# A decode-layer backward kernel: six V slots of its own, reloaded once their V is transposed, and more side-product steps per head after head 52

## The chip, the cores and the metric

The kernel runs on one core of a Trainium2 chip. The metric is device time in microseconds (us) of that core. Each kernel was run several times; executions of one kernel mostly agree within 0.3%, and comparisons carry a 95% interval.

## The reference, cut to what matters

The reference is one transformer layer at decode (one query per sequence) with its gradients: layer norm, attention over a cache of 4096 keys, output projection, gated MLP. There are 4 x 32 = 128 heads, and each has a K and a V of 4096 x 128 in bfloat16, 1 MiB each. What counts here is the backward part of attention:

```python
q = (x @ wq).reshape(B, Sq, H, Dh).transpose(0, 2, 1, 3)
scores = einsum("bhqd,bhkd->bhqk", q, k_cache) * Dh**-0.5
p = softmax(scores); o = einsum("bhqk,bhkd->bhqd", p, v_cache)
# gradients, per head (dO is the gradient of o, c = sum(dO * o)):
#   grad_V = outer(p, dO)                                1 MiB out
#   dP = V @ dO                                          V is read a second time
#   grad_K = outer(p * (dP - c) * scale, q)              1 MiB out
# side products: gradients of wq, wo, w1, w2, w3 and x, some 15 MB out
```

So the backward part moves 1 MiB in and 2 MiB out per head, and little arithmetic goes with it.

## The kernel before

On-chip memory holds 22 slots of 128 x 4160 bfloat16, kept in a queue `free`. Every large thing takes the slot at the head of the queue and gives it back at the tail when the program order is done with it; the framework adds the waits.

```python
class Slot:
    def __init__(self, name):
        self.i = free.popleft()
        self.t = slotp.tile([P, SLOT], BF16, name=name, tag=f"slot{self.i}")
    def give(self):
        free.append(self.i)
```

In the backward loop TensorE transposes a V in four groups of eight blocks, ScalarE evicts them, and TensorE makes dP. VectorE makes the outer products; GpSimd issues the stores, SyncE the loads:

```python
def V_T(s, ps):
    VTs[s] = Slot("VT")
    VT, Vn = VTs[s].heads(), V2s[s].heads()
    for g in range(SJ // GW):                       # 4 groups
        pt = ps.tile([P, GW, P], BF16, tag="tps", name="pt_tps")
        for i in range(GW):
            nc.tensor.transpose(pt[:, i, :], Vn[:, g * GW + i, :], ident_b[:])
        nc.scalar.copy(out=VT[:, g * GW:(g + 1) * GW, :], in_=pt[:])
    V2s.pop(s).give()

def load_V2():
    s = nv["next"]
    if s < NH:
        V2s[s] = Slot("V2")
        nc.sync.dma_start(out=V2s[s].heads(), in_=cache_head(A_v_cache, s))
        nv["next"] += 1

def front(s):                                       # cut
    ...
    V_T(s, psT)
    for j in range(SJ):
        nc.tensor.matmul(dP_ps[:, j:j + 1], lhsT=VT[:, j, :], rhs=dOT_bf[:, s:s + 1], start=True, stop=True)
    VTs.pop(s).give()
    P_pairs(s + 1)                                  # a copy on GpSimd

def grad_V(s):
    gv = Slot("gv")
    outer(gv.heads(), P2s.pop(s), reps["rdo", s // REP][:, s % REP, :])     # VectorE
    nc.gpsimd.dma_start(out=rows_of(out_3[b, h]), in_=gv.heads())
    gv.give()
# grad_K(s): dSt, dS2 on VectorE, then gk in the same way to out_2

def prefetch(s):
    while nv["next"] < min(NH, s + 10) and len(free) > 8:
        load_V2()

for s in range(NH):
    prefetch(s + 1)
    if s + 1 < NH:
        if s + 1 not in V2s and s + 1 not in VTs:
            load_V2()
        front(s + 1)
        grad_V(s + 1)
    grad_K(s)
    if s < S0:                                      # S0 = 8
        step("o")                                   # rest of dO
    else:
        step("s", 1 if s < S0 + 44 else 2 + (s % 4 == 0))     # side products
step("s", 400)
```

The side products are a generator; one step is one small matmul with its eviction, and every eighth or so a store. A part of it:

```python
oflat = Slot("oflat")
for b in range(B):
    nc.gpsimd.dma_start(out=oflat.b(HD)[b:b + 1, :], in_=O_sb[b::B, :])     # four tiny transfers
for _ in range(6):
    yield
for h0 in range(0, H, 8):                           # grad of wo, uses oflat
    ...
```

## Time and profile before

| | before |
|---|---|
| time, median of the first three runs | 1743.66 us |
| profiled execution | 1740.73 us (span 1739.0) |
| bytes moved | 707.86 MB, mean 407 GB/s |
| backward loop | from about 720 us to the end |
| TensorE, VectorE, ScalarE busy | 76%, 72%, 55% |

How to read what follows. "DMA" is a row of tenths (busy share of the 16 DMA engines per slice), "GB/s" what they moved. A line of the view of stretches names a stretch in us from the start, its length, busy time of TensorE, weight loads, VectorE, ScalarE and GpSimd with counts, and at the end the granted TensorE clock, the DMA share and GB/s. A line of the view of waits reads: engine and line that waited, what it waited for, total us, how often, the longest. A line of the issues names the transfer, its queue, how many, the size, and the median us from issue to landing. The prediction below shows the views of the kernel before.

### The profile page before, as it was taken

Reading aid. Unit: us, or ns where it says so; the run is one execution under the profiler, and the core shown is the slowest. Engines: PE = TensorE matmul, PEld = TensorE weight load, DVE = VectorE, ACT = ScalarE, POOL = GpSimd, SP = SyncE. Lnnn points to the kernel's source line nnn. Section 1 sums busy time; section 2 is a strip of 40 time slices with the busy share of each in tenths; the row PEclk is TensorE's granted clock in tenths of the full one; section 3 lists DMA queues with packets and bytes.
Section 4 is the critical chain, followed back from the end, with each engine's and each line's share of the span. In section 5 each row is a group of like instructions: output and inputs, shape, how many; then the busy total and the mean of one; then the engine's idle time right before and its main releaser. Section 6 shows DMA issues by size and latency. Waiting matters only on the chain.

```text
span 1739.0 us, 44055 instructions
## 1 busy us (share of the span) xinstructions
PE 1321.9 (76%) x18996; PEld 1113.4 (64%) x18996; DVE 1250.8 (72%) x1385; ACT 955.6 (55%) x1464; POOL 508.2 (29%) x815
## 2 busy tenths in 40 slices
PE   5889888888888888888777767777577667656675
PEld 4667666676666667777667666655466455545564
DVE  5989999889998996675666576656566465656665
ACT  3455445444444444765545445576367566656675
POOL 2333333333333331231222232212223232223332
PEclk8999999999999999765655565586555655656555
DMA  9999999999999999799999999999999999999998
GB/s 398 410 419 418 419 418 419 419 413 418 419 414 399 417 406 396 312 403 421 420 420 416 419 419 413 408 423 423 413 389 396 409 401 409 403 413 403 415 407 328
DMA packets 107043, 707.86 MB, mean 407 GB/s; under 512 B 11024, under 2 KB 18840, under 8 KB 23904
## 3 DMA queue, kind: packets, MB, share of 16 engines
q1 hardware_dynamic: 66880, 422.60, 59.9%
q0 software_dynamic: 39968, 282.44, 39.3%
q8 instruction: 149, 2.44, 0.5%
q14 instruction: 46, 0.38, 0.1%
HBM read 422.58 MB, written 282.34 MB: 405 GB/s over the span
## 4 chain that ended last, share of the span: by engine, by line
DMA 37%; DVE 9%; issue 5%; PE 5%; ACT 4%; POOL 2%; DVEq 0%; POOLq 0%; ACTq 0%; SPq 0%
DMA out_dram<-gv 21%; DMA out_dram<-gk 13%; DVE gk L1091 5%; DVE gv L1091 3%; ACT VT L759 3%; PE pt_tps L758 2%; POOL P L1075 2%; DMA out_dram<-gwq 1%; DMA wo<-in_A_wo_dram 1%; DMA V<-in_A_v_cache_dram 1%; PE gps L886 0%; PE dP_ps L1085 0%; DVE PK L421 0%; PE rep_ps L1063 0%; DVE dS L1112 0%
## 5 line engine op out<-in xcount | busy, mean ns | idle before, releaser
L759 ACT COPY VT<-pt_tps 128x1024 bf16<-128x1024 bf16 x512 | 492.7, 1015 | 247.6 <-PE pt_tps L758 166.7
L758 PE MATMUL pt_tps<-ident_b,V 128*128 128x128 bf16 x4096 | 453.9, 294 | 122.2 <-ACT VT L759 119.1
L758 PEld LDWEIGHTS <-V 128*128 128x128 bf16 x4096 | 402.5, 138 | 202.1 <-issue 180.7
L1091 DVE TENSOR_TENSOR gv<-P,reps 128x4096 bf16<-128x4096 bf16 x128 | 292.9, 2289 | 198.2 <-DMA out_dram<-gv 141.0
L1091 DVE TENSOR_TENSOR gk<-dS,reps 128x4096 bf16<-128x4096 bf16 x128 | 293.4, 2292 | 145.2 <-DMA out_dram<-gv 86.7
L421 DVE TENSOR_TENSOR PK<-Kn,PK 128x4096 bf16<-128x4096 bf16 x128 | 302.9, 2366 | 35.2 <-POOL PK L417 34.8
L436 PE MATMUL M_ps<-PK,Vn 128*128 128x130 bf16 x4096 | 285.9, 222 | 42.6 <-DMA Vn<-in_A_v_cache_dram 42.5
L436 PEld LDWEIGHTS <-Vn 128*128 128x128 bf16 x4096 | 253.2, 99 | 62.6 <-DMA Vn<-in_A_v_cache_dram 55.3
L328 DVE STREAM_TRANSPOSE KT<-Kn 128x512 f32<-128x512 f32 (+1 forms) x321 | 250.9, 798 | 0.5 <-issue 0.5
L323 ACT COPY KT<-pt_tps 128x1024 bf16<-128x1024 bf16 x128 | 129.4, 1012 | 187.1 <-PE pt_tps L322 154.7
L1085 PE MATMUL dP_ps<-dOT_bf,VT 128*128 128x1 bf16 x4096 | 146.5, 166 | 107.8 <-DVE dSt L1109 55.8
L1085 PEld LDWEIGHTS <-VT 128*128 128x128 bf16 x4096 | 139.1, 104 | 121.5 <-ACT VT L759 60.7
L1116 POOL DMA_DIRECT2D out_dram<-gk x128 | 68.2, 532 | 429.2 <-DVE gk L1091 414.0
L417 POOL COPY PK<-P_all 128x64 bf16<-128x64 bf16 x128 | 32.3, 252 | 437.0 <-ACT P_all L411 411.8
L336 POOL COPY zq<-qT_bf 128x2 bf16<-128x2 bf16 x128 | 152.1, 1189 | 0.0
L1102 POOL DMA_DIRECT2D out_dram<-gv x128 | 68.5, 535 | 269.0 <-DVE dSt L1109 251.7
L1075 POOL COPY P<-P_all 128x64 bf16<-128x64 bf16 x128 | 133.8, 1046 | 0.0
L411 ACT COPY P_all<-pt_P 32x64 bf16<-32x64 bf16 x256 | 51.9, 203 | 57.5 <-PE pt_P L407 55.3
L322 PE MATMUL pt_tps<-ident_b,Kn 128*128 128x128 bf16 x1024 | 80.6, 223 | 0.7 <-DVE qrep L282 0.7
L446 PE MATMUL kP_ps<-PK,onesw 128*32 128x512 bf16 x1024 | 79.6, 388 | 0.0
L322 PEld LDWEIGHTS <-Kn 128*128 128x128 bf16 x1024 | 62.2, 100 | 26.5 <-issue 26.4
L400 ACT ACTIVATE Pn<-E,rl 128x1024 bf16<-128x1024 f32 x64 | 73.7, 1151 | 2.8 <-DVE rl L397 2.8
(227 smaller groups left out, 1299.8 us busy)
## 6 DMA issues: line engine op xcount, KB each, us to landing
Kn<-in_A_k_cache_dram SPq DMA_DIRECT2D x128, 1024.0 KB, 14.8
Vn<-in_A_v_cache_dram SPq DMA_DIRECT2D x128, 1024.0 KB, 14.9
V<-in_A_v_cache_dram SPq DMA_DIRECT2D x128, 1024.0 KB, 13.5
out_dram<-gv POOLq DMA_DIRECT2D x128, 1024.0 KB, 15.9
out_dram<-gk POOLq DMA_DIRECT2D x128, 1024.0 KB, 16.2
wq<-in_A_wq_dram SPq DMA_DIRECT2D x8, 1024.0 KB, 12.6
out_dram<-gw POOLq DMA_DIRECT2D x6, 896.0 KB, 19.3
wo<-in_A_wo_dram SPq DMA_DIRECT2D x4, 1024.0 KB, 12.0
```

The costliest lines, as they stand in the source:

```text
L322: nc.tensor.transpose(pt[:, i, :], Kn[:, c * GW + i, :], ident_b[:])
L323: nc.scalar.copy(out=KT[:, c * GW:(c + 1) * GW, :], in_=pt[:])
L328: nc.vector.transpose(out=KT[:, c * w_:(c + n) * w_], in_=Kn[:, c * w_:(c + n) * w_])
L336: nc.gpsimd.tensor_copy(out=zq[gi % 2][hl][:, 32:132:67], in_=qT_bf[:, s:s + 1].to_broadcast([P, 2]))
L421: nc.vector.tensor_tensor(out=PK[:, :, 0:Dh].rearrange("p j (r t) -> p j r t", t=2), in0=Ks[s].heads().rearrange("p j (r t) -> p j r t", t=2),
L436: nc.tensor.matmul(hold["M"][:], lhsT=Vn[:, j, :], rhs=PK[:, j, :], start=(j == 0), stop=(j == SJ - 1))
L446: nc.tensor.matmul(hold["kP"][32 * q:32 * (q + 1), :, :], lhsT=ones_window(w), rhs=PK[:, j0:j0 + 4, 0:Dh], start=(w == 0 and c == 0), stop ...
L758: nc.tensor.transpose(pt[:, i, :], Vn[:, g * GW + i, :], ident_b[:])
L759: nc.scalar.copy(out=VT[:, g * GW:(g + 1) * GW, :], in_=pt[:])
L1075: nc.gpsimd.tensor_copy(out=P2s[s][:], in_=P_all[:, s, :, None].to_broadcast([P, SJ, 2]))
L1085: nc.tensor.matmul(dP_ps[:, j:j + 1], lhsT=VT[:, j, :], rhs=dOT_bf[:, s:s + 1], start=True, stop=True)
L1091: nc.vector.tensor_tensor(out=dst.rearrange("p j (r t) -> p j r t", t=2), in0=col2[:, :, None, :].to_broadcast([P, SJ, Dh // 2, 2]), in1=r ...
```

## The change

The intent: a V should be loaded as soon as an earlier V has been transposed, not when some output store has left a slot. So six slots become a ring for V alone, and all others rotate among outputs. The step rate of the side products rises from 2.25 to 2.75 per head after head 52, so that they end earlier.

```diff
     class Slot:
-        def __init__(self, name):
-            self.i = free.popleft()
+        def __init__(self, name, src=free):
+            self.i = src.popleft()
             self.t = slotp.tile([P, SLOT], BF16, name=name, tag=f"slot{self.i}")
@@ V_T
-        V2s.pop(s).give()
+        sl = V2s.pop(s)
+        (vring if len(V2s) + len(vring) < NV2 else free).append(sl.i)
@@
+    NV2 = 6
+    vring = deque()
     nv = {"next": 0}
     def load_V2():
         s = nv["next"]
         if s < NH:
-            V2s[s] = Slot("V2")
+            V2s[s] = Slot("V2", vring if vring else free)
@@
-        def prefetch(s):
-            while nv["next"] < min(NH, s + 10) and len(free) > 8:
+        def prefetch():
+            while nv["next"] < NH and vring:
                 load_V2()
@@
-            prefetch(s + 1)
+            prefetch()
@@
-                step("s", 1 if s < S0 + 44 else 2 + (s % 4 == 0))
+                step("s", 1 if s < S0 + 44 else 2 + (s % 4 < 3))
```

## The prediction

> **What bounds the kernel now.** I read the page first. Its second part shows DMA at nine tenths in nearly every slice while no compute engine is near full, so the 16 DMA engines are the bound; the interest is in the row below, what they moved. The total is 707.86 MB, and the change moves the same bytes. The slices are 43.5 us each; the backward loop over heads starts in the 17th (about 720 us).
>
> ```profile
> DMA  9999999999999999799999999999999999999998
> GB/s 398 410 419 418 419 418 419 419 413 418 419 414 399 417 406 396 312 403 421 420 420 416 419 419 413 408 423 423 413 389 396 409 401 409 403 413 403 415 407 328
> ```
>
> The first row cannot rank the slices; the second can: about 420 GB/s when the queues are full, 389 to 409 in most slices from the 30th on, 328 in the last. So the engines count as busy while some of them have nothing to take. I then cut the backward part into stages (view of chosen stretches; last three columns are granted clock, DMA share, GB/s):
>
> ```profile
> 720.00:760.00 40.00, 31.91 (x507) 28.86 (x506) 30.57 (x25) 29.36 (x32) 14.51 (x19) 0.63 0.91 362
> 760.00:1240.00 480.00, 356.44 (x4487) 323.80 (x4484) 296.09 (x246) 270.33 (x297) 123.70 (x185) 0.59 1.01 419
> 1240.00:1660.00 420.00, 282.70 (x3384) 225.19 (x3383) 256.73 (x216) 254.46 (x319) 123.10 (x170) 0.57 1.00 404
> 1660.00:1740.00 80.00, 53.55 (x666) 44.07 (x663) 47.63 (x40) 49.97 (x61) 21.71 (x31) 0.56 0.89 359
> ```
>
> The stage of 480 us is at the DMA limit already. The other three are below it, and what can be won lies there. Why they are below is in the waits of the load queue (whole run), where line 768 is the second load of V:
>
> ```profile
> SPq L768 <- DMA out_dram<-gk: 510.3, 49, 38.7
> SPq L768 <- DMA out_dram<-gw: 116.3, 5, 24.6
> SPq L768 <- DMA out_dram<-gv: 115.4, 14, 23.0
> SPq L768 <- DMA out_dram<-gwq: 67.6, 3, 24.6
> SPq L768 <- PE pt_tps L758: 20.5, 19, 6.0
> ```
>
> A V load waits some 810 us in all for an output store to leave the slot it is given, and only 20.5 us for the transposes of an earlier V. The longest wait, 38.7 us, is at the start: between 720 and 740 us the DMA view has no read at all and moves 6.67 MB. The compute side waits for the same stores (view of waits, whole run):
>
> ```profile
> DVE gv L1091 <- DMA out_dram<-gv: 141.0, 35, 7.7
> DVE gk L1091 <- DMA out_dram<-gk: 52.0, 26, 2.4
> ACT VT L759 <- DMA out_dram<-gk: 42.6, 10, 12.6
> ACT gw L880 <- DMA out_dram<-gk: 26.1, 5, 10.2
> ```
>
> The VectorE waits cost nothing while other stores are still being moved. The ScalarE ones can: when ScalarE stands 12.6 us for a VT slot, nothing is produced behind it. In the timeline this one ends at 1398.9 us; the next stores are issued only from 1405 us, and the DMA strip of 1400 to 1420 us falls to 371 GB/s.
>
> **What the Trainium skill says.** "DMA: Bandwidth & Descriptors", section on the anatomy of one DMA (SWDGE path): DMA engines do not wait on semaphores; any wait happens on the issuing sequencer before dispatch. The trace agrees: the waits above stand on the queue of SyncE, and a V load that waits holds up those behind it. Same page, "Issuing engines are not separate DMA queues": loads from SyncE and stores from GpSimd share the 16 engines and interleave. It agrees: between 1120 and 1240 us the two together make 423 GB/s, where loads alone made 418 to 419 in the forward part: no second path. Same page, "Specifications": a fabric ceiling of 435 GB/s and an HBM limit per core of about 358. The trace stays below the first and contradicts the second (407 GB/s mean), so 420 is near the most there is. "Perfetto Trace Analysis", "Optimization Strategy": repeated bubbles on the engine that should be full can mean too few buffers. Here they do: 22 slots are shared.
>
> **The change part by part.** No instruction and no byte is added or removed; the forward part and the first eight V loads stay the same. So everything before about 725 us is unchanged.
>
> 1. *The V ring.* I followed the slot lists of both programs in program order. Before, the rule "more than 8 free" keeps nine slots in rotation, and from head 8 on over half of the V loads (66 of 115) get a slot whose last user was an output store; in heads 0 to 7 the rule lets only one V be loaded (the ninth), with four more just before head 8. After, every load from the ninth on takes the slot of a V that has been transposed, five to six heads ahead. The 810 us of waits of the load queue should nearly go. By themselves they are not time: they count where the engines starved.
> 2. *The output slots.* Before, an allocation of gv or gk that has to wait for a store has some 3.5 to 4 younger stores behind it. After, the slots outside the ring all rotate, and that number is about 2 in heads 0 to 7 (worse than 2.7), 3.7 in heads 8 to 15 (equal), 5 in 16 to 35, and 6 to 9 afterwards. So when a wait ends, 6 to 9 MB are still on the way (14 to 21 us at 421 GB/s) where it was 4 MB (10 us). That covers a stop like the 6 us between wait and next store above.
> 3. *Side products.* The step rate goes from 2.25 to 2.75 per head from head 52. The last gwo takes its slot at head 109 instead of 121, so the last heads have only their own work. Per head the rate adds half a step, about 0.3 us of ScalarE (590 ns per gwo eviction). ScalarE per head: 4 x 1.015 us for VT, 0.3 for reps, 2.75 x 0.55 for steps = 5.9 us. VectorE: 2 x 2.29 + 0.245 + 0.226 = 5.05 us. DMA: 3 x 1.0486 MB at 421 GB/s = 7.5 us. There is room, so this part is not a cost.
>
> Sum, by stage. The DMA time lost is stretch x (1 - rate / full rate):
> - 720 to 760: 40 x (1 - 362/421) = 5.6 us lost. The ninth load waits until the third V is transposed, some 8 to 10 us in, and output slots are tight. I take 3 us back.
> - 760 to 1240: at 419, nothing (the best part of it made 423; deeper queues might give 1 to 3 us).
> - 1240 to 1660: 420 x (1 - 404/419) = 15 us lost. Some stays: the stretch 1260 to 1280 has 1923 packets under 2 KB, and loads of weights still wait in the same queue. I take 11 to 12 us back.
> - 1660 to the end of the stores (1732): 28.7 MB in 72 us, 68 us at 421. In this tail each head took about 6.4 us with the gwo steps, against 2.1 MB / 421 = 5 us of stores. Without steps I expect about 5.3 us (the rate of the first heads: 7 gk in 40 us is 5.7 with other side work), and a backlog of 8 stores hides the rest. I take 4 us back.
> Together 18 to 19 us, plus about 2 for the deeper queue in the middle: 1743.7 - 21 = 1722 us.
>
> **Rivals.**
> A. *Full saturation.* From 720 us to the end 414 MB are moved (406 GB/s x 1020 us). At 422 to 425 throughout, they take 974 to 981 us; against 1012 used, that is 31 to 38 us less: 1706 to 1713. For it: 423 over 120 us, and the last stores alone run at about 430 (5.26 MB in the 12.3 us after 1720). Against: the early heads and the small packets.
> B. *Output slots become the bound early.* With six slots tied to V, eight held by the M sums and three by wo, four are left for VT, gv and gk in heads 0 to 7, and seven until head 13 or so. A gk waits for the gv of one head before. With a store of L us from issue to landing, and one gv and one gk (4.6 us) per step, a head takes about (L + 4.6) / 2: 7.5 us needs L = 10.4. Stores took 5.6 us there without reads and 15 to 18 with full queues. If the ring's reads stretch L to 14, a head takes 9.3 us, 1.8 us too much over some 8 heads: 15 us lost, and the time would be about 1737. Against it: if the engines starve, L shrinks, so it corrects itself.
> C. *The reads were hidden anyway.* The engines are full through most of it, and if the bubbles after 1240 us come from side products taking slots rather than from V, only start and tail are won: 7 us, 1737.
> D. *Compute takes over.* TensorE runs at a granted clock of 0.5 to 0.6 and takes turns with ScalarE on the transposes. At 6.4 us per head in the tail and half a step more, about 6.9, it stays under 7.5. I hold this unlikely.
>
> **Range and chances.** Main line 1722; A pulls to 1708, B and C to 1737. I take 1709 to 1736. Faster by over 2% needs less than about 1709, 35 us won, hardly without A in full: 0.08. Slower by over 2% has no mechanism of that size: 0.01. Within: 0.91.
>
> **What would show it.** Right: the load queue's waits for out_dram fall from about 810 to under 100 us and turn to TensorE's transposes; reads appear before 735 us; the stretch that was 404 is at 415 or more; the last 70 us before the end keep above 415; stores take longer from issue to landing (20 us or more instead of 16). Wrong: the stretch after 1240 stays near 404 (C); the first 60 us of the loop fall under 380 with VectorE waiting for gv (B); the DMA share falls under 0.95 in the middle (D).

## The result and the profile after

The changed kernel took 1736.69 us (median of 4 runs, 1734.48 to 1739.39), the kernel before 1743.98 us (median of 4, 1742.89 to 1746.05). The ratio is 0.9958, 95% interval 0.994 to 0.9975. The gain is real and small, about 7 us where 21 were predicted. In two more rounds of runs, both on one chip (e0 and e16 below), the same kernel came to 0.9983 (0.9964 to 1.0003) and 0.9972 (0.9953 to 0.999). So it is worth 3 to 7 us, and 1736.69 lies just above the stated range.

The profiled execution of the changed kernel took 1739.39 us, the slowest of its four, and that of before 1740.73, faster than its timed ones. The two traces therefore differ by less than the kernels do; I use them for where time moved. First the page's rows of the changed kernel:

```profile
DMA  9999999999999999899999999999999999999997
GB/s 397 410 418 418 419 418 419 419 412 418 418 415 397 418 407 396 321 388 416 414 413 415 417 412 416 422 423 423 419 412 418 414 414 414 373 400 408 410 419 315
```

The slices of 389 to 409 that began with the 30th are gone up to the 34th, as meant: from the 19th to the 34th slice the rate is 412 to 423. After that come one hole (373, the 35th), three slices of 400 to 410, and a last slice of 315. By stage, in the same stretches as in the prediction:

```profile
720.00:760.00 40.00, 29.62 (x379) 26.48 (x378) 26.72 (x22) 26.76 (x29) 13.75 (x17) 0.54 0.96 384
760.00:1240.00 480.00, 364.24 (x4620) 328.56 (x4620) 312.67 (x266) 274.95 (x304) 127.58 (x194) 0.59 1.01 415
1240.00:1660.00 420.00, 298.01 (x3573) 235.68 (x3572) 248.87 (x204) 273.85 (x347) 110.28 (x167) 0.58 1.00 408
1660.00:1740.00 80.00, 33.07 (x471) 30.25 (x468) 44.51 (x36) 28.18 (x30) 16.76 (x28) 0.57 0.85 350
```

The start gained (362 to 384), the middle lost (419 to 415), the stage after 1240 us gained a third of what was expected (404 to 408), and the last one moved less (359 to 350). Then the load queue, whole run (cut to these lines; waits of the forward part and of the program's end are left out):

```profile
SPq L773 <- PE pt_tps L758: 835.1, 116, 19.8
SPq L925 <- DMA out_dram<-gv: 23.0, 2, 15.3
SPq L502 <- DMA out_dram<-gk: 16.1, 1, 16.1
SPq L925 <- DMA out_dram<-gk: 13.9, 1, 13.9
```

Line 773 is the V load (768 before). It waits for TensorE's transposes and for no store; the three waits for stores are those of weight loads. So the mechanism works as told. The stores have a deeper backlog; the time from issue to landing in the kernel before and in the changed one:

```profile
out_dram<-gv POOLq DMA_DIRECT2D x128, 1024.0 KB, 15.9
out_dram<-gk POOLq DMA_DIRECT2D x128, 1024.0 KB, 16.2
```

```profile
out_dram<-gv POOLq DMA_DIRECT2D x128, 1024.0 KB, 24.5
out_dram<-gk POOLq DMA_DIRECT2D x128, 1024.0 KB, 24.0
```

Some 8 us longer: more stores are on the way. Counted in the trace from issues and landings, 7.4 of GpSimd's transfers are under way on average from 1340 to 1490 us, where it was 4.4. And GpSimd, which issues them, now waits for earlier stores to land (view of waits of GpSimd; the largest such wait before was 5.2 us in total):

```profile
POOL out_dram L1107 <- DMA out_dram<-gv: 53.2, 21, 4.7
POOL out_dram L1121 <- DMA out_dram<-gk: 49.3, 20, 4.1
POOL out_dram L1121 <- DMA out_dram<-gv: 26.8, 9, 4.7
POOL out_dram L1107 <- DMA out_dram<-gk: 13.1, 6, 4.1
```

The program's waits tell why: its transfers take eight semaphores in turn, so each of GpSimd's transfers waits for the eighth one back. In both traces the stores' semaphores (99 to 106) come round in order, and never more than eight of GpSimd's transfers are under way.

Last the end of both traces, the DMA strip of 1720 to 1740 us (half a microsecond per digit), before and after:

```profile
DMA  9998989999999999999899999411000000000000
```

```profile
DMA  9999899797664533323111000000000000000000
```

Before, all engines stop together. After, they fall out one by one over some 6 us. The trace has sixteen landings for each transfer, one per DMA engine, without the engine's number. Those of the last store:

| last store lands (us) | first engine | mean of 16 | last engine |
|---|---|---|---|
| before | 1732.8 | 1733.4 | 1735.1 |
| changed | 1723.4 | 1727.5 | 1733.7 |

The mean engine is done 5.9 us earlier, the last one 1.4 us. The experiments below turn on this.

A second thing is in the trace's packet records. A packet of 8192 bytes mostly takes 309 ns (16 engines at that pace make 424 GB/s). From 1340 to 1500 us the mean load packet took 350.7 ns before and 314.9 after (my reading: the loads no longer start into empty queues). But the mean store packet went from 312.4 to 320.0 ns, and of all stores from 720 us on, 743 packets (329 before) took over 550 ns, with a median of 606. Summed over the loop and divided by 16 engines, what packets of 8192 bytes took above 309 ns is, in us:

| | loads | stores | together |
|---|---|---|---|
| before | 17.2 | 12.8 | 30.0 |
| changed | 5.2 | 22.8 | 28.0 |

The loads gave back 12 us, and the stores took 10 of them.

### The profile page after: what moved, and what is told of

Same layout as the page of the kernel before. It is cut to its first block, busy times and chain, and to the rows that moved or that the text cites. A ratio compares the mean times of both kernels' runs of the same rounds, so it can differ in the third digit from the quotient of the medians.

```text
span 1737.6 us, 43932 instructions
## 1 busy us (share of the span) xinstructions
PE 1324.3 (76%) x18996; PEld 1114.6 (64%) x18996; DVE 1252.8 (72%) x1385; ACT 955.0 (55%) x1464; POOL 493.6 (28%) x815
## 4 chain that ended last, share of the span: by engine, by line
DMA 43%; DVE 5%; ACT 4%; PE 3%; issue 2%; POOL 1%; POOLq 0%; DVEq 0%; ACTq 0%
DMA out_dram<-gk 20%; DMA out_dram<-gv 18%; ACT VT L759 3%; DMA V<-in_A_v_cache_dram 3%; DVE gk L1096 2%; DVE gv L1096 2%; PE pt_tps L758 2%; DMA out_dram<-gw 2%; DMA oflat<-O_sb 1%; PE gps L891 1%; POOL P L1080 0%; PE dP_ps L1090 0%; ACT reps L1071 0%; PE rep_ps L1068 0%; ACT gwo L885 0%
## 5 line engine op out<-in xcount | busy, mean ns | idle before, releaser
L1090 PE MATMUL dP_ps<-dOT_bf,VT 128*128 128x1 bf16 x4096 | 152.1, 166 | 73.4 <-ACT VT L759 63.5
L1080 POOL COPY P<-P_all 128x64 bf16<-128x64 bf16 x128 | 119.2, 932 | 0.0
## 6 DMA issues: line engine op xcount, KB each, us to landing
out_dram<-gv POOLq DMA_DIRECT2D x128, 1024.0 KB, 24.5
```

The costliest lines, as they stand in the source:

```text
L1080: nc.gpsimd.tensor_copy(out=P2s[s][:], in_=P_all[:, s, :, None].to_broadcast([P, SJ, 2]))
```

## The experiments

My theory after the result had two parts: compute and issue stalls that are left in the changed kernel (a hole at 1500 us), and a limit of the engines with deep store queues. The rivals were that the gain came from the tail alone, or that the depth itself does harm. Each row below has 5 or 6 timed runs, but for e14 (4) and e12 (2); "before" is the kernel before on the same chip.

| run | edit | median us | before | ratio (95%) |
|---|---|---|---|---|
| e1_ring_only | ring, old step rate | 1735.91 | 1743.23 | 0.9960 (0.9945 to 0.9974) |
| e2_side_only | old rule, new step rate | 1743.17 | 1743.23 | 0.9994 (0.998 to 1.0008) |
| e3_oflat16 | oflat used 16 steps later | 1739.56 | 1743.23 | 0.9975 (0.9963 to 0.9988) |
| e4_thin_compute | changed, a quarter of the transposes | 1729.40 | 1743.23 | 0.9923 (0.9909 to 0.9938) |
| e0_after_again | changed kernel | 1741.33 | 1743.52 | 0.9983 (0.9964 to 1.0003) |
| e5_park4 | 11 output slots for 15 | 1738.79 | 1743.52 | 0.9970 (0.9958 to 0.9982) |
| e6_threes | V loads by threes | 1738.02 | 1743.52 | 0.9971 (0.9958 to 0.9984) |
| e7_ring3 | ring of 3 | 1745.26 | 1743.52 | 1.0003 (0.999 to 1.0016) |
| e8_oflat_sp | e3, tiny loads from SyncE | 1735.42 | 1744.63 | 0.9949 (0.9936 to 0.9962) |
| e10_thin_before | before, a quarter of the transposes | 1731.93 | 1744.63 | 0.9931 (0.9916 to 0.9945) |
| e12_quarter_V | e4, a quarter of each V loaded | 1511.44 | 1744.63 | 0.8664 (0.8648 to 0.8681) |
| e13_ring_late | e8, ring from head 52 on | 1737.62 | 1743.86 | 0.9963 (0.9951 to 0.9976) |
| e14_thin_ring_late | e13, a quarter of the transposes | 1728.93 | 1743.86 | 0.9912 (0.9897 to 0.9927) |
| e16_after_third | changed kernel | 1737.31 | 1742.85 | 0.9972 (0.9953 to 0.999) |
| e17_oflat_sp_again | e8 | 1736.27 | 1742.85 | 0.9961 (0.9945 to 0.9977) |
| e15_shallow_end | e8, 6 output slots from head 108 | 1738.13 | 1742.85 | 0.9968 (0.9955 to 0.9981) |

**e1_ring_only and e2_side_only** do one part of the change each: the first has `2 + (s % 4 == 0)` in the changed kernel, the second `2 + (s % 4 < 3)` in the kernel before.

> The changed kernel with the old step rate of the side products (2.25 per head). Theory 'ring': the gain of 7 us comes from V no longer waiting for stores and the faster side products give nothing or cost a little; then this is at 1733 to 1738, and the stall of TensorE on oflat (14.2 us in the changed kernel) is shorter, as 6 steps last 2.7 heads instead of 2.2. Rival 'tail': the gain is the tail without side products; then this is at 1740 to 1744.

> The kernel before with only the faster step rate. Theory 'ring': no gain, 1742 to 1746. Rival 'tail': most of the gain, 1735 to 1740, with the last 70 us at over 410 GB/s.

The ring alone has the whole gain, and the faster side products alone have none. The rival "tail" is out.

**e3_oflat16** takes away the largest single stall of the changed kernel, the wait of TensorE for the tiny loads of oflat:

```profile
PE gps L891 <- DMA oflat<-O_sb: 14.2, 1, 14.2
```

```diff
-            for _ in range(6):
+            for _ in range(16):
                 yield
```

> The changed kernel with 16 steps instead of 6 between the load of oflat and its first use. Theory 'compute stalls': the wait of TensorE for oflat (14.2 us, with 326 GB/s from 1500 to 1520 us) starves the DMA engines and costs about 4.5 us; without it 1732, and no 20 us stretch between 1400 and 1660 under 390 GB/s. Rival 'backlog': the time is set by how fast the engines move what is queued, and the lost 4 us come back elsewhere; then 1735 to 1738.

A miss: 1739.56 us lies above the ranges of both theories. TensorE's wait is gone, but the stretch from 1500 to 1520 us still moves only 368 GB/s (326 in the changed kernel), and the time is no better. The timeline of GpSimd in e3 shows what else stands there:

```profile
1492.65 0.72 POOL L1014 DMA_DIRECT2D out_dram<-gw  x1
1494.64 0.55 POOL L1024 DMA_DIRECT2D oflat<-O_sb  x1 [1.27 <-DMA out_dram<-gw]
1496.79 0.52 POOL L1024 DMA_DIRECT2D oflat<-O_sb  x1 [1.61 <-DMA out_dram<-gv]
1499.34 0.53 POOL L1024 DMA_DIRECT2D oflat<-O_sb  x1 [2.02 <-DMA out_dram<-gk]
1503.43 0.52 POOL L1024 DMA_DIRECT2D oflat<-O_sb  x1 [3.56 <-DMA out_dram<-gv]
1503.94 0.25 POOL L1080 COPY P<-P_all 128x64 bf16<-128x64 bf16 x1
1507.89 0.57 POOL L1107 DMA_DIRECT2D out_dram<-gv  x1 [3.69 <-DMA out_dram<-gk]
```

(Start, duration, instruction, and in brackets what ended the idle time before it.) Each of the four 8 KB loads waits for a store to land, then counts as one of eight transfers under way. For 15 us no store is issued, the backlog halves, and the copy of P that VectorE needs stands behind them.

**e4_thin_compute** asks what the time would be if compute were no matter. It transposes only the first quarter of each V and takes dP from that (wrong K gradients: relative error 1.2); all transfers stay.

```diff
-        for g in range(SJ // GW):
+        for g in range(1):
@@
-                ... lhsT=VT[:, j, :], ...
+                ... lhsT=VT[:, j % GW, :], ...
```

> Wrong results for K and V gradients on purpose: each V is transposed only in its first quarter and dP taken from that, so ScalarE and TensorE do a quarter of that work and all transfers stay. Theory 'compute stalls': with compute out of the way the engines stay full at 421 GB/s and the time falls to 1715 to 1722. Theory 'backlog': the engines are slower with many stores and a V load side by side (8 KB store packets of 606 ns instead of 309), whatever compute does; then 1730 to 1736.

With ScalarE's work in the stretch from 1240 to 1660 us halved (124.74 us busy for 273.85), 1729.4 is all: 7 us above the range of "compute stalls" and 0.6 us below that of "backlog". So "backlog" came nearer, but compute is not free either: thinning it took some 7 us off the changed kernel. The 421 GB/s of the prediction were not reached in this order (417 and 416 in the two long stretches).

**e0_after_again, e5_park4, e6_threes, e7_ring3** went to one chip, to vary depth and rhythm. The edits: in e5, `if s % MC == MC - 1 and s // MC >= 4` before the M slots are given; in e6, `if len(vring) >= 3 or nv["next"] >= NH - 3` before the loop of loads; in e7, `NV2 = 3`.

> The changed kernel once more, on the chip of the three below, so that they can be compared with it and its spread is known: 1735 to 1740.

> The changed kernel with four of the slots of the M sums never given back, so that 11 instead of 15 slots rotate and some 4 to 5 instead of 6 to 9 stores are on the way. Theory 'depth harms': the deep backlog lets the 16 engines drift apart (a store's first and last engine land 10 us apart at the end, 2.3 us in the kernel before) and stretches store packets; with less of it the drift falls to 5 us, and the time to 1728 to 1733. Rival 'depth is neutral': once the engines are full more depth changes nothing; 1735 to 1740. Rival 'depth helps': bubbles return as in the kernel before, 1740 or more.

> The changed kernel with the same ring, but three V loads issued together each third head, so that the load queue runs empty and starts again a third as often. Theory 'restart': store packets are stretched (606 ns instead of 309) around the moment a V load starts beside full store queues, once per head; a third of the starts saves 5 to 8 of the 10 us that they cost more than before: 1729 to 1733. Rival 'mix': it is the number of stores side by side with reads, not the starts; 1735 to 1740.

> The changed kernel with a ring of 3 V slots instead of 6: V is loaded two to three heads ahead, and 18 slots rotate for the rest; seven instead of four output slots in the first eight heads. Theory 'early slots': the first 80 us (360 GB/s from 760 to 780 us) were short of output slots; 2 to 4 us better, 1732 to 1735. Theory 'depth harms': worse or equal, 1736 to 1741. If V then comes late behind the weight loads in the same queue, TensorE waits for V and it is slower still.

The changed kernel spread from 1735.08 to 1746.06 here, so differences of 3 us can't be told from it. e5 took the backlog back (stores land after 17.2 us for 24.5) at no change of time: depth is neutral. The drift that "depth harms" expected to fall to 5 us was still 9.1 us in the last store. In e6 the sum above 309 ns stayed (7.3 us loads, 20.9 stores): "restart" falls. e7 shows no gain over the kernel before (1.0003), and "early slots" (1732 to 1735) falls: its first 40 us of the loop run at 354 GB/s (384), so fewer V ahead and more output slots early did not help, and my worry about too few output slots in the first heads (rival B) finds no support. Its interval overlaps that of e0, so that it is slower than the changed kernel is not shown.

**e8_oflat_sp** moves the tiny loads to the other queue, on top of e3:

```diff
-                nc.gpsimd.dma_start(out=oflat.b(HD)[b:b + 1, :], in_=O_sb[b::B, :])
+                nc.sync.dma_start(out=oflat.b(HD)[b:b + 1, :], in_=O_sb[b::B, :])
```

(and the same for dqflat).

> The changed kernel with the eight tiny loads of dqflat and oflat moved from GpSimd's queue to SyncE's, and 16 steps before oflat is used. Theory 'GpSimd blocks': GpSimd never has more than eight transfers under way, and with a full backlog the four tiny loads stand for four of them, so that the stores behind them come late; that is why taking away TensorE's wait alone (16 steps) gave nothing. Without both, no 20 us stretch from 1400 to 1660 under 395 GB/s and 4 us less than the changed kernel: 1732 to 1735. Rival 'the lost time only moves': 1736 to 1741.

Its stretches:

```profile
760.00:1240.00 480.00, 356.74 (x4612) 320.11 (x4610) 311.19 (x265) 274.51 (x302) 123.64 (x191) 0.61 1.01 415
1240.00:1660.00 420.00, 301.11 (x3561) 237.69 (x3560) 253.02 (x205) 273.14 (x347) 113.49 (x167) 0.58 1.01 415
1660.00:1740.00 80.00, 33.96 (x494) 31.30 (x492) 42.35 (x35) 29.80 (x32) 20.36 (x25) 0.56 0.77 321
```

The hole is closed and the late stage is at 415, just what the prediction wanted there. 420 x (415/404 - 1) = 11.4 us should have come of it against the kernel before. They did, for the mean engine: in e8's last store the mean landing is at 1721.5 us (1733.4 before). The last engine lands at 1731.0 us (1735.1 before). GpSimd as the cause of the hole is shown; that closing it shortens the kernel is not (e8 is below e3 on the same chip, 0.9949 to 0.9975, but e17, its repeat on the other chip, came to 0.9961).

**e10_thin_before** thins the kernel before as e4 does the changed one.

> The kernel before with the same thinned compute as e4 (wrong K gradients on purpose). It tells what the order of transfers and the slots are worth when compute is out of the way; the changed kernel came to 1729.4 so. Theory 'compute stalls made the ring worth something': then without them both orders are the same, 1728 to 1732. Theory 'reads late': V behind the stores costs by itself, and this stays 6 to 14 us above, 1735 to 1743.

1731.93 us: with compute out of the way the old order is 12 us faster than with it, and about as fast as the ring. Its load queue still waits 732 us for output stores (476.8 + 137.9 + 117.6). So late V loads cost little by themselves. That the ring, with full compute, makes compute stalls cost less is my reading; no run shows it directly.

**e12_quarter_V** loads only the quarter of V that e4 uses, so that stores run nearly alone.

> The thinned changed kernel with only a quarter of each V loaded a second time (the quarter that is used; K gradients wrong on purpose), so that 96 MB of 402 fall away from the backward part and stores run nearly alone. A measurement of the stores by themselves: theory 'mix' (store packets are stretched because reads run beside them) expects them at 425 GB/s or more and 1495 to 1505; rival 'stores are slow by themselves': 412 to 418 GB/s, 1505 to 1520, with the tail of the engines as ragged as before.

By its numbers the rival came true: 1511.44 us, 412 GB/s from 760 to 1060 us, and a ragged end. But it doesn't decide on the rate, for the quarter loads have short rows (2 KB instead of 8), so that many more small packets run beside the stores. On the packets it speaks for "mix": 99 stores over 550 ns instead of 513 in e4, and a mean of 314.0 ns instead of 317.2. In these two runs, long store packets come mostly where full V loads run beside them. The engines drift apart all the same (8.0 us in the last store).

**e13_ring_late and e14_thin_ring_late** take the old rule up to head 51 and the ring after it, with full and with thinned compute.

```diff
-        (vring if len(V2s) + len(vring) < NV2 else free).append(sl.i)
+        (vring if s >= SW and len(V2s) + len(vring) < NV2 else free).append(sl.i)
@@
-            while nv["next"] < NH and vring:
+            while nv["next"] < NH and (vring or s < SW and nv["next"] < s + 10 and len(free) > 8):
```

> e8 with the old rule for V up to head 51 (V loads share all slots) and the ring of six only from head 52. Theory 'ring costs in the middle': with the ring the stretch of 760 to 1240 us ran at 412 to 416 GB/s where the kernel before had 419, some 4 us; with the old rule there and the ring after it both are had: 419 and 415, and 1730 to 1733, better than both kernels and than e8 (1735.4). Rival 'the floor is what it is': 1734 to 1738.

> The same with the thinned compute of e4 and e10 (K gradients wrong on purpose): a third order of the same transfers with compute out of the way, after 1729.4 (ring) and 1731.9 (old rule). If the floor of some 1730 belongs to the transfers and not to their order, 1726 to 1732 again; if the two orders each lost something of their own, 1719 to 1725.

e13 missed its 1730 to 1733: it kept 418 GB/s from 760 to 1100 us (412 in the changed kernel) and 416 after 1240, but fell to 407 (422) between them, where the rules change, and ended at 1737.62 us. The two middle stretches of e14:

```profile
760.00:1240.00 480.00, 219.94 (x3063) 187.59 (x3064) 307.20 (x260) 101.37 (x120) 136.61 (x188) 0.51 1.01 418
1240.00:1660.00 420.00, 169.98 (x2269) 109.48 (x2269) 246.91 (x199) 123.29 (x186) 109.44 (x165) 0.51 1.01 419
```

418 and 419, together the best of all kernels, and yet 1728.93 us. Its last store lands on the first engine at 1710.5 us, on the mean at 1713.8, on the last at 1723.9. Three orders of the same transfers, with compute thinned, end at ratios of 0.9923, 0.9931 and 0.9912, with overlapping intervals: in these three orders alike some 12 to 15 us under the kernel before, which looks like a floor.

**e16_after_third, e17_oflat_sp_again, e15_shallow_end**, on one chip, ask whether the lag of one engine sets the end, or whether the drift is a loss of its own.

```diff
             prefetch()
+            if s == 108:
+                parked = [free.popleft() for _ in range(9)]
```

> The changed kernel on the chip of the next two, to compare with: 1735 to 1741.

> e8 again beside the changed kernel on one chip. Theory 'GpSimd blocks': 3 to 5 us below the changed kernel. Rival 'the lost time only moves': within 1.5 us of it.

> e8 with nine of the fifteen slots outside the ring taken out of use from head 108 on, so that some three stores instead of eight are on the way over the last 20 heads. In e8 the last stores land with their first and last engine more than 10 us apart and the last 12 us run at a third of the rate. Theory 'slowest engine': one engine has fallen behind and sets the end; fewer stores make the end sharp (first and last under 5 us apart), the faster engines wait before instead of after, and the time stays within 2 us of e8. Rival 'drift is a loss of its own': the end comes 4 to 6 us earlier than in e8.

The DMA strip of 1720 to 1740 us, e17 and then e15:

```profile
DMA  4533313211111000000000000000000000000000
```

```profile
DMA  9998999989999799998120000000000000000000
```

In e17 fewer than half the engines work at 1720 us; in e15 all do. Last store in e17: first engine 1717.1, mean 1721.4, last 1731.1 us. In e15: 1729.7, 1730.2, 1732.1. With few stores under way the fast engines have to wait before the end, not after it, and the end stays: 1738.13 for 1736.27 us, as "slowest engine" expected. The drift is how the lag shows; making the queue shallow did not win it back.

The last store alone misleads, though. The median time between a store's first and last landing, by stage, and in brackets how many of GpSimd's transfers are under way on average (us):

| | 900 to 1240 | 1340 to 1490 | 1520 to 1560 | last store |
|---|---|---|---|---|
| before | 7.8 | 7.4 (4.4) | 7.3 | 2.3 |
| changed | 8.9 | 17.6 (7.4) | 6.8 | 10.3 |
| e5 | 7.2 | 8.6 (5.0) | 8.0 | 9.1 |
| e17 | 8.9 | 16.3 (7.4) | 16.8 | 14.0 |
| e15 | 9.7 | 17.3 (7.4) | 16.9 | 2.4 |

The engines of the kernel before are apart too, all through the loop; they come together only in the last heads. (e2, with the old rule, ends 8.6 us apart in the same time as the kernel before.) And the hole at 1500 us was where the changed kernel's last engine caught up, 17.6 to 6.8 us. In e17 the hole is closed, the spread stays at 16.8, and the last engine ends only 2.6 us earlier (1731.1 for 1733.7), the mean one 6.1. That would explain why a stretch at 415 GB/s did not become time. e17 against the changed kernel is 1736.27 to 1737.31, inside their spread; e8 is the best version found and beats the kernel before on both chips, but it is not shown to beat the changed kernel.

What stays open: which engine lags and why, and whether it is the same one throughout. The packet and landing records carry no engine number. Nor is it shown why store packets take 606 ns beside V loads, or whether the lagging engine has more of them.

## Why the prediction was right or wrong

**The bound and the mechanism: right.** The loop is bound by transfers, though compute costs 7 us of the changed kernel and 12 of the kernel before (e4, e10). The V loads stopped waiting for stores, the queue turned to TensorE's transposes, reads came before 735 us (2.09 MB between 720 and 740 us), stores take longer to land, and the side products' pace alone is worth nothing (e2). No rival about compute taking over (D) came true.

**The step that failed: "1 - rate / full rate" as time won.** The sum took the mean rate of 16 engines in each stage and turned each GB/s into time at the end. In these runs the end came with the last engine. Of the prediction's 21 us (its terms, 18 to 19 and about 2, make 20 to 21, so 1723 to 1724 rather than 1722) the changed kernel's trace shows 5.9 us for the mean engine and 1.4 for the last; even in e8 it is 11.9 us for the mean (1733.4 to 1721.5) and 4.1 for the last. With more stores under way the engines spread further (7.4 us at 4.4 stores before, 17.6 at 7.4 changed, from 1340 to 1490 us): the fast ones run ahead and lift the mean, and the lagging one gains less. This account rests on e8, e17 and e15, one trace each; what makes an engine lag is not shown. With compute thinned, three orders end near 1730 us, and no run of the full transfers came under 1726.85: nothing here says that 1722 could be had.

**By the terms of the sum:**

- *Start, 3 us taken.* 720 to 760 us went from 362 to 384 GB/s, 2.1 us at 421. But 760 to 780 us fell from 418 to 360, 2.8 us back. Together nothing.
- *Middle, 0 and perhaps 2 us more from deeper queues.* It lost: 419 to 415, or 480 x 4/419 = 4.6 us. I had taken a fuller queue to be a faster one; from 760 to 1100 us the runs with the ring moved 412 or 413 GB/s (changed, e1, e8), those with the old rule there 418 or 419 (before, e2, e13). Store packets beside V loads were longer (321.4 ns for 317.4 from 780 to 1100 us).
- *1240 to 1660, 11 to 12 us.* 404 to 408, 4 us. The step did not count a limit that only the deeper backlog reaches: eight transfers of GpSimd under way. With that put right (e8) the stretch gets its 415 and the 11.4 us of the mean engine.
- *Tail, 4 us.* Nothing: the sharp end of the kernel before became a ragged one, 10.3 us between the first and last engine.

**Rivals.** A (full saturation) was the farthest off, and its evidence, 423 GB/s over 120 us, was again a mean over engines. B was real for 20 us only. C gave the right number, 1737, by luck: it saw the gain in start and tail, and these gave nothing. On the reads it was not far off, for e10 shows that late V loads cost little by themselves. The range was too narrow because A, B and C all varied how full the engines are, and none asked what a full set of engines can do.

**What the skill said, once more.** "Issuing engines are not separate DMA queues" held. That a wait stands on the issuing sequencer, not on the DMA engine, I had applied to SyncE alone; the runs showed it on GpSimd too (the four waits above, 142 us together).

## What to carry to other kernels

Where the transfer engines are the bound, do not take a gain in the mean rate of a stage for time won (11.9 us against 4.1 in e8): compare the landing of the first and the last engine at the end, and try the floor by thinning compute while keeping every transfer. Before deepening a queue, look for the next limit on what may be under way (here eight transfers of one issuing engine), and keep tiny transfers out of that queue. A freed queue is worth what its waits cost in idle engines, and 810 us of waits were worth 3 to 7 us here.

## What the Trainium skill lacked or had wrong

- "DMA: Bandwidth & Descriptors", "Specifications": an HBM limit of about 358 GB/s per core, which the same row derives as half of a stack's 716. The runs of one core show 407 GB/s over the whole kernel and 423 over 120 us of the kernel before. The skill's other pages already allow a single core more, so this is a row to be reworded; the prediction was too quick to call it contradicted.
- The same page, "Latency and other measured facts", says that two of the engines are usually slower than the others and gives a guess at the cause; further on it says that a bulk load goes at the pace of its slowest engine. It lacks how far the engines drift apart over many transfers: 7.4 us between a store's first and last landing with 4.4 stores under way, 17.6 with 7.4, and 10 to 14 at the end of the changed kernel and e17. Whether it is the two engines that the page means, no run here shows.
- No page has that store packets of 8192 bytes take about 606 ns instead of 309 in part beside a load stream (743 over 550 ns of 33,052 in the changed kernel, 99 with a quarter of the loads and thinned compute, 513 with thinned compute alone).
- "Perfetto Trace Analysis", "Optimization Strategy", on repeated bubbles and too few buffers: true here, but it lacks a warning that closing them need not pay. Load bubbles shrank from 17.2 to 5.2 us of engine time, and store packets grew from 12.8 to 22.8.
